# Where weight chunks are staged and when they are requested, added and rooted, in a threshold-attention and feed-forward kernel

## The chip, the cores and the metric

The kernel runs on one core of a Trainium2 chip. The metric is the device time of one execution in microseconds; several executions are taken and their median is given. A profile of one execution stands beside them. Engines are called as the profile calls them: PE (TensorE), DVE (VectorE), ACT (ScalarE), POOL (GpSimd), SP (the engine that issues most transfers). "PEld" is the loading of weights into PE.

## The reference, cut to what matters

```python
# attention: q, k, v are (8, 8, 576, 64) float32, tau a scalar
scores = 1.0 / sqrt(64) * q @ k.transpose(0, 1, 3, 2)
thresh = max(scores, axis=-1) - tau
scores = where(scores >= thresh, scores, -1e9) - max
attn = exp(scores) / (sum(exp(scores)) + 1e-9)
x = (attn @ v), heads joined to (8, 576, 512)
# feed-forward: w_ch1 is (512, 2048), w_ch2 (2048, 512)
mu, var = mean(x), mean((x - mu) ** 2)
xn = (x - mu) / sqrt(var + 1e-6) * g_ln
out = x + maximum(xn @ w_ch1, 0) @ w_ch2
```

The two weight matrices arrive as float64. [...] the kernel takes each value's two 32-bit words apart and makes a float32 of them.

## The kernel before

**Slots.** Attention is done in slots. A batch has 8 heads, two to a partition set, and 9 slots: four for the first 256 rows of each pair of heads, one for the last 64 rows of all, four for the second 256 rows. The loop at L1078 passes 72 slots, numbered n; batch 0 is slots 0 to 8. In a slot PE makes the scores (L402), DVE takes the row maxima (`neg`, L416), POOL the thresholds (`thr`, L420), ACT the exponentials (L429), DVE compares with the threshold, multiplies and sums (L436), and POOL divides by the sum (L452). From slot 6 on (`FIRST`), DVE turns the weights in blocks (L526 for most slots) and SP stores them to DRAM (`scr<-et`, L533 in batch 0, L537 later) and reads them back turned (`em<-scr`, L547, later L551) at the start of the next slot. PE multiplies them with v in part 3 of that next slot (L595, L605). ACT copies these products to `x` (L618) and POOL adds the features up (`sum`, L647) one slot later.

**Feed-forward.** Tokens go in 16 groups of 288. A group's first part makes 16 tiles of `hidden` (`p`, L788, by the helper at L101), each with a relu on ACT (L793). The second part is plain for group 0 (L824, 64 products in four outputs m) and done in seven half-size segments for the others. Two PSUM tiles tagged "ff" take turns for these products, so a product waits for the relu or copy of the last but one. The norm's factor comes from a variance (`var`, L807), Ln and Exp on ACT (L809 to L811), and a correction step on DVE, `root` (L731), which is put on a list `aside` and issued when the list is emptied. Its two scratch tiles in group 0 are `sq[:, 2]` and `sq[:, 3]`, which are tiles 14 and 15 of `hidden`; at L783 `first_part` empties the list before tile 14 is made.

**Order.** The order of every queue is written out by the program: each engine does its instructions in the order in which this Python code issues them. A slot has four places where `second_part` (L999) issues feed-forward steps. It issues as many as fit a share worked out from what is still to be done, and it stops where a weight chunk has not been "carried" yet (L781, L822). POOL's scaling of q (L335) is issued in `turn` (L340), which DVE's transposes of q and k for the next slot belong to.

**Conversion.** `Weights` (L177) brings in 32 chunks of 128 x 512 values, 512 KB each; 0 to 15 belong to w_ch1, 16 to 31 to w_ch2. A chunk goes through these steps:

- `fetch`: SP requests the raw words (L259) into a free piece of SBUF. Pieces lie in regions that are used otherwise later: the unfilled part of `w2`, `hidden`, `x_room`, `y_room`, `et_room`, `stage`, and `e_room[1]`. A piece carries a limit: it may be taken by chunk i only if its limit is above i. Of those that fit, the one with the lowest limit is taken. `wait` says how many ticks ago the piece must have been given back.
- `prepare_to`: ACT writes Abs of the high words to the chunk's final place (L275), and Copies of the low words (L280).
- `begin`: DVE does three masks (L290, L293, L297).
- `carry`: POOL adds the low part (L305) and, for w_ch1, multiplies by g (L308). `carry_all` does this for all chunks begun, last first.

`BEGUN` (L1054) gives for each slot the counts of chunks to be begun after the maxima, after the weights, and at the slot's end. In slot 8, `conversion.fetch(3, ...)` at L1095 requests chunks 29 to 31 early in the slot, ahead of `load_qk` (L1108) and of the store in `turn_blocks` (L1138). At a slot's end, `begin_to(end_at)` and `carry_all()` stand together (L1175, L1176), ahead of the next slot's maxima and thresholds.

Of the kernel before, what the change touches and what calls it, by code (L numbers as in the profile page):

```python
# [8 lines left out]
F32 = mybir.dt.float32  # L9
# [4 lines left out]
AF = mybir.ActivationFunctionType  # L14
# [4 lines left out]
def kernel(  # L19
# [31 lines left out]
    nc = tc.nc  # L51
# [6 lines left out]
    ND = DF // 128  # L58
# [15 lines left out]
    ffn = ctx.enter_context(tc.tile_pool(name="ffn", bufs=2))  # L74
# [6 lines left out]
    eps_sb = consts.tile([128, 1], F32, name="eps_sb")  # L81
# [4 lines left out]
    w2_sb = consts.tile([128, NK, ND, 128], F32, name="w2")  # L86
# [88 lines left out]
    WC = 512  # L175

    class Weights:  # L177
# [13 lines left out]
        def __init__(self):  # L191
            self.chunks = [
                (w1_sb[i][:, c : c + WC], w_ch1[i * 128 : (i + 1) * 128, c : c + WC], i)
                for c in range(0, DF, WC)
                for i in range(NK)
            ] + [
                (
                    w2_sb[:, m, d : d + 4].rearrange("p d c -> p (d c)"),
                    w_ch2[d * 128 : (d + 4) * 128, m * 128 : (m + 1) * 128].rearrange(
                        "(d p) c -> p d c", p=128  # L200
                    ),
                    None,
                )
                for m in range(NK)
                for d in range(0, ND, 4)
            ]
            self.n1 = NK * (DF // WC)
            self.fetched = self.prepared = self.converted = self.begun = self.carried = 0
            self.raw, self.ticks = {}, 2
            flat = lambda t: t.rearrange("p a b -> p (a b)")  # L210

            x_room = ffn.tile([128, NK, TOK], F32, tag="x", bufs=3, name="x_room")
            y_room = ffn.tile([128, NK, TOK], F32, tag="sq", bufs=1, name="y_room")
            et_room = att.tile([128, NB, 128], F32, tag="et", bufs=1, name="et_room")
            stage = self.stage = consts.tile([128, 8, WC], F32, name="stage")

            n1 = self.n1  # L220
            self.free = []
            for t, n, before in (
                (w2_sb.rearrange("p m d c -> p (m d) c"), ND // 2, lambda p: n1 + 2 * p - 6),
                (hidden, 4, lambda p: 10),
                (x_room, 1, lambda p: 2 * n1),
                (y_room, 1, lambda p: 2 * n1),
                (et_room, 2, lambda p: n1 - 3),
                (stage, 4, lambda p: 2 * n1),
            ):
                for p in range(n):  # L230
                    self.free.append((before(p), -1, flat(t)[:, p * 2 * WC : (p + 1) * 2 * WC]))

        def take(self, t):
            t = t.rearrange("p a b -> p (a b)")
            for p in range(2):
                self.free.append((2 * self.n1, -1, t[:, p * 2 * WC : (p + 1) * 2 * WC]))

        def piece(self, i, wait):

# [21 lines left out]
                )  # L261

        def give(self, got):
            self.free.append((got[0], self.ticks, got[2]))

        def words(self, i, t):
            return self.raw[i][2].bitcast(t).rearrange("p (n two) -> p n two", two=2)
# [1 line left out]
        def prepare_to(self, most, lows=True):  # L269

            new = range(self.prepared, max(self.prepared, min(most, self.fetched)))
            for i in new:
                assert all(self.raw[j][0] + 6 > i or self.raw[j][0] == 10 for j in range(self.carried, i))
                dst, top = self.chunks[i][0], self.words(i, F32)[:, :, 1]
                nc.scalar.activation(dst, top, func=AF.Abs)  # L275
            self.prepared = max(self.prepared, min(most, self.fetched))
            while self.converted < (self.prepared if lows else self.begun):
                low, low_in = self.words(self.converted, I32), self.words(self.converted, U32)
                self.converted += 1
                nc.scalar.activation(  # L280
                    low[:, :, 0], low_in[:, :, 0], func=AF.Copy, scale=2.0**-29
                )
# [43 lines left out]
    FIRST = HP + 2  # L326
# [350 lines left out]
    aside, stores, drops = [], [], []  # L677
# [53 lines left out]
    def root(y, x, t):  # L731


        nc.vector.scalar_tensor_tensor(
            out=t, in0=y, scalar=-0.5, in1=y, op0=ALU.mult, op1=ALU.mult
        )
        nc.vector.tensor_mul(t, t, x)
        nc.vector.scalar_tensor_tensor(out=y, in0=t, scalar=1.5, in1=y, op0=ALU.add, op1=ALU.mult)
        rooted.append(y)

    rooted = []
    HT, HD, HM = TOK // 2, ND // 2, NK // 2
# [30 lines left out]
    def first_part(g):  # L773


        xc = centred.pop(g)
        rb = sq = None
        plain = g == 0
        sums_of = differences() if g == 1 else iter(())
        for d in range(ND):  # L780
            while conversion.carried < 4 * (d // 4 + 1):  # L781
                yield 0, 0
            while d == ND - 2 and len(rooted) <= g:  # L783
                run_all(aside)
            p1 = ps_ff.tile([128, TOK], F32, tag="ff", name="p1")
            for c in range(NK):
                product(
                    p1, lhsT=w1_sb[c][:, d * 128 : (d + 1) * 128], rhs=xc[:, c],  # L788
                    start=(c == 0), stop=(c == NK - 1),
                )  # L790
                if c < NK - 1:
                    yield 1, 1
            nc.scalar.activation(hidden[:, d], p1, func=AF.Relu)  # L793
            next(sums_of, None)
            yield 2, 1
            if sq is None and d and (part > 1 or d == ND // 2 - 1):
                squared = d
                sq = hidden[:, ND - NK :]
                nc.scalar.activation(sq, xc, func=AF.Square)
                for c in range(1, NK):  # L800
                    nc.gpsimd.tensor_tensor(out=sq[:, 0], in0=sq[:, 0], in1=sq[:, c], op=ALU.add)
            elif sq is not None and rb is None and (
                d >= squared + (7 if plain else 3) and part > (0 if plain else 1)
                or d == ND - NK - 1
            ):
                var = ps_ff.tile([128, TOK], F32, tag="ff", name="var")
                product(var, lhsT=avg_sb, rhs=sq[:, 0], start=True, stop=True)  # L807
                rb = ffn.tile([128, TOK], F32, tag="rb", bufs=2, name="rb")
                nc.scalar.activation(sq[:, 2], var, func=AF.Identity, bias=eps_sb)  # L809
                nc.scalar.activation(rb, sq[:, 2], func=AF.Ln)  # L810
                nc.scalar.activation(rb, rb, func=AF.Exp, scale=-0.5)  # L811
                aside.append(lambda: root(rb, sq[:, 2], sq[:, 3]))
                yield 1, 1
        for _ in sums_of:
            pass
        return rb
# [171 lines left out]
    def run(n, i):  # L988
        for fn, args in later_calls.pop((n, i), ()):
            fn(*args)  # L990
# [48 lines left out]
    conversion = Weights()  # L1039
    if w_ch1.dtype == I64:  # L1040
        conversion.fetch(2)
    else:
# [10 lines left out]

    BEGUN = [  # L1054
        (0, 0, 1), (2, 2, 3), (4, 4, 5), (6, 6, 7), (8, 8, 9), (10, 10, 11),
        (13, 16, 19), (21, 23, 24), (26, 27, 29), (31, 32, 32), (32, 32, 32),
    ]

    def constants(times):
# [18 lines left out]
    for n in range(NS):  # L1078
# [9 lines left out]
            scale_q(n + 1, loaded[n + 1][0])  # L1088
        rest = exponentials(n)
        es, thr = next(rest)  # L1090
        run(n, 0)
        if n == HP + 2:
            next(rest, None)
        if n >= HP:
            conversion.fetch(3, -1 if n > FIRST else 1)  # L1095
        run_first(stores)
        if n == FIRST:
            convert(masks_at)
# [34 lines left out]
            conversion.carry_all()  # L1133
        box = []
        if blocks_go:
            conversion.fetch(3, wait=0)
            conversion.prepare_to(end_at, False)
            scr = turn_blocks(b, s, es)  # L1138
            if n == FIRST:
                conversion.take(e_room[1])  # L1140
                conversion.fetch(2)
            conversion.carry_all()
            at_quarter(n + 1, 0, lambda b=b, s=s, scr=scr, box=box: box.append(fetch(b, s, scr)))
        else:

            made = turn_weights(s, es, diags)
            for i, at in enumerate(
                (-1, -1, 0, 0)
            ):
                if i == 3 and n + 1 == FIRST:  # L1150
                    at_quarter(n + 1, 0, conversion.prepare_to, BEGUN[n + 1][0], False)
                if i < 3:
                    at_quarter(n + 1, at, next, made)
                else:
                    at_quarter(n + 1, at, lambda made=made, box=box: box.append(next(made)))
# [17 lines left out]
            conversion.prepare_to(BEGUN[n + 1][0] - (n == FIRST - 1))  # L1173
        second_part(n, 3)
        conversion.begin_to(end_at)  # L1175
        conversion.carry_all()  # L1176
        if FIRST <= n < SLOTS:
            conversion.prepare_to(BEGUN[n + 1][0], False)
        if not plain_at(n):
# [42 lines left out]
```

## Time and profile before

| what | value |
|---|---|
| median of 3 runs | 1347.89 us (1347.65 to 1348.77) |
| the profiled execution's own time | 1348.64 us |
| its span in the profile | 1346.9 us |
| mean granted PE clock | 0.995 |
| busy shares of the span | PE 98%, PEld 74%, DVE 65%, ACT 34%, POOL 46% |
| transfers | 213.92 MB, mean 159 GB/s |

The span is the time from the first to the last instruction in the profile, and the execution's own time has 1.7 us around it. A share is an average over the whole span. The conversion of weights lies in the first 160 us of it, where the shares are others; times below count from the span's start. In a row of the timeline the columns are the start in us, the length in us, the engine, the line and operation, output and inputs, and the count of merged instructions; in brackets is the idle time before it and what ended that. In a list of waits they are total us, how often, and the longest. In a table by stretches each engine has its busy us and, in brackets, its instructions.

### The profile page before, as it was taken

To read this page: it belongs to the slowest core of one execution; us is meant where nothing else is said; L and a number is where in the kernel's file an instruction comes from. 1 tells how busy PE (TensorE), PEld (TensorE's weight loads), DVE (VectorE), ACT (ScalarE), POOL (GpSimd) and SP (SyncE) were. 2 spreads that over 40 slices of the span, in tenths; PEclk is the share of its full clock that TensorE was granted. 3 is DMA by queue.
4 is the path that set the end of the run, shared out by engine and by line. 5 is a ranking of instruction groups with operands and counts; after the bars stand their busy time and mean duration, and the time that the engine had idled before them with its cause. 6 is when DMAs were issued, how large, how long until landed. Compare 5 with 4: busy or idle time off the path is not lost.

```text
span 1346.9 us, 40264 instructions
## 1 busy us (share of the span) xinstructions
PE 1315.2 (98%) x17304; PEld 990.6 (74%) x17304; DVE 873.9 (65%) x1544; ACT 458.8 (34%) x995; POOL 624.9 (46%) x836
## 2 busy tenths in 40 slices
PE   8898899999999999999999999999999999999997
PEld 7665557769686786968778696877869677786957
DVE  7899786667666675666756677556756667666112
ACT  5875233232423233232233324233232323323120
POOL 3567456535444444444534454443444445335313
PEclk9999899999999999999999999999999999999999
DMA  8927864557643775447644576447754376443211
GB/s 164 302 75 202 207 176 163 178 150 193 179 150 120 193 200 159 151 156 192 172 149 151 166 179 191 142 143 193 197 171 151 121 199 180 133 156 124 85 19 20
DMA packets 335298, 213.92 MB, mean 159 GB/s; under 512 B 247376, under 2 KB 292688, under 8 KB 327056
## 3 DMA queue, kind: packets, MB, share of 16 engines
q1 hardware_dynamic: 329008, 210.46, 54.5%
q8 instruction: 136, 2.23, 0.7%
q10 hardware_dynamic: 5952, 0.74, 0.4%
q14 instruction: 42, 0.34, 0.1%
q0 software_dynamic: 160, 0.15, 0.1%
HBM read 124.00 MB, written 87.29 MB: 157 GB/s over the span
## 4 chain that ended last, share of the span: by engine, by line
PE 89%; DVE 4%; ACT 2%; DMA 2%; SPq 1%; issue 1%; POOL 1%; ACTq 0%; POOLq 0%; DVEq 0%
PE p L101 36%; PE seg L101 31%; PE sc L402 10%; PE sc L595 8%; PE sc L605 2%; ACT e L429 1%; DVE e L436 1%; PE tp L101 1%; SPq L118 1%; DVE w L297 1%; PE var L101 1%; PE mean L101 1%; DVE neg L416 0%; DMA em<-scr 0%; DVE w L293 0%
## 5 line engine op out<-in xcount | busy, mean ns | idle before, releaser
L101 PE MATMUL p<-xc,w 128*64 128x288 f32 x4096 | 518.9, 409 | 8.4 <-ACT part L880 4.6
L101 PEld LDWEIGHTS p<-xc,w 128*64 128x64 f32 x4096 | 287.4, 137 | 217.8 <-issue 14.9
L416 DVE TENSOR_REDUCE neg<-sc 128x2 f32<-128x1152 f32 x144 | 188.8, 1352 | 286.1 <-PE sc L402 285.6
L452 POOL TENSOR_SCALAR e<-e,den 128x576 f32<-128x576 f32 x264 | 205.8, 792 | 131.3 <-DVE den L441 131.3
L101 PE MATMUL seg<-hidden,w 128*64 128x144 f32 x3840 | 247.9, 287 | 0.0
L101 PEld LDWEIGHTS seg<-hidden,w 128*64 128x64 f32 x3840 | 234.8, 137 | 11.5 <-issue 8.5
L436 DVE SCALAR_TENSOR_TENSOR e<-sc,thr,e 128x576 f32<-128x576 f32 x288 | 222.5, 810 | 19.2 <-POOL thr L420 11.6
L420 POOL TENSOR_SCALAR thr<-neg,low_sb 128x2 f32<-128x2 f32 x144 | 40.3, 280 | 382.6 <-DVE neg L416 381.6
L793 ACT ACTIVATE hidden<-p 128x288 f32<-128x288 f32 x256 | 106.5, 416 | 303.3 <-PE p L101 302.2
L429 ACT ACTIVATE e<-sc,neg 128x576 f32<-128x576 f32 x288 | 197.4, 753 | 2.4 <-DVE neg L416 2.4
L526 DVE STREAM_TRANSPOSE et<-e 128x1152 f32<-128x1152 f32 x118 | 161.0, 1372 | 14.2 <-POOL e L452 13.7
L402 PE MATMUL sc<-kT,qT 64*64 64x384 f32 (+3 forms) x2048 | 140.3, 404 | 2.5 <-DVE e L436 1.6
L595 PE MATMUL sc<-em,v_in 128*64 128x128 f32 (+1 forms) x2368 | 131.5, 265 | 5.9 <-DMA em<-scr 2.8
L595 PEld LDWEIGHTS sc<-em,v_in 128*64 128x64 f32 x2368 | 124.1, 138 | 14.5 <-DVE w L297 3.0
L101 PE MATMUL seg<-hidden,stage 128*64 128x144 f32 x1920 | 123.3, 287 | 0.0
L101 PEld LDWEIGHTS seg<-hidden,stage 128*64 128x64 f32 x1920 | 117.6, 137 | 2.9 <-issue 2.9
L618 ACT COPY x<-sc 128x128 f32<-128x128 f32 x120 | 31.6, 265 | 247.2 <-PE sc L402 175.9
L865 POOL TENSOR_TENSOR hidden<-hidden 128x576 f32<-128x576 f32 x60 | 84.8, 1428 | 52.0 <-ACT hidden L793 42.4
L402 PEld LDWEIGHTS sc<-kT,qT 64*64 64x64 f32 x2048 | 76.3, 133 | 44.1 <-issue 21.3
L880 ACT COPY part<-seg 128x288 f32<-128x288 f32 x74 | 29.8, 403 | 190.6 <-PE seg L101 190.1
L865 DVE TENSOR_TENSOR hidden<-hidden 128x576 f32<-128x576 f32 x60 | 51.2, 887 | 51.5 <-PE seg L101 48.5
L101 PE MATMUL seg<-hidden,e 128*64 128x144 f32 x896 | 61.2, 286 | 0.0
(125 smaller groups left out, 1048.0 us busy)
## 6 DMA issues: line engine op xcount, KB each, us to landing
scr<-et SPq DMA_DIRECT2D x63, 1152.0 KB, 5.0
em<-scr SPq DMA_DIRECT2D x63, 1024.0 KB, 5.8
out_dram<-ot SPq DMA_DIRECT2D x248, 36.0 KB, 3.7
q_in<-in_q_dram SPq DMA_DIRECT2D x120, 72.0 KB, 2.8
er<-scr SPq DMA_DIRECT2D x132, 64.0 KB, 5.1
k_in<-in_k_dram SPq DMA_DIRECT2D x116, 72.0 KB, 3.0
v_in<-in_v_dram SPq DMA_DIRECT2D x28, 256.0 KB, 5.5
w<-in_moe_w_ch_dram SPq DMA_DIRECT2D x10, 512.0 KB, 8.3
```

Of the source, the lines that this page charges most:

```text
L101: nc.tensor.matmul(out[r], lhsT=lhsT[:, r], rhs=rhs, **flags)
L402: nc.tensor.matmul(sc[h][64 * i : 64 * i + 64, at : at + n], lhsT=ql[r] if s == HP else qT[r, half, j * 128 + 64 * i : j * 128 + 64 * i + 64],
L416: nc.vector.tensor_reduce(out=neg[:, i], in_=pairs[h], axis=AXL.X, op=ALU.max, negate=True,)
L420: nc.gpsimd.tensor_scalar(out=thr[:, i], in0=neg[:, i], scalar1=-1.0, scalar2=low_sb, op0=ALU.mult, op1=ALU.add,)
L429: nc.scalar.activation(es[:, i], blocks[i], func=AF.Exp, bias=neg[:, i : i + 1])
L436: nc.vector.scalar_tensor_tensor(out=es[:, i], in0=blocks[i], scalar=thr[:, i : i + 1], in1=es[:, i], op0=ALU.is_ge, op1=ALU.mult, accum_o ...
L452: nc.gpsimd.tensor_scalar(out=es[:, i], in0=es[:, i], scalar1=den[:, i : i + 1], scalar2=1.0, op0=ALU.mult, op1=ALU.mult,)
L526: nc.vector.transpose(et[:, :, 64 * h : 64 * h + 64].rearrange("p n (j c) -> p j n c", j=2), es[:, 2 * h : 2 * h + 2].rearrange("p j (n c) ...
L595: nc.tensor.matmul(dst[64 * h : 64 * h + 64], lhsT=vt[:, h, c, :], rhs=pick(em[:, 2 * j : 2 * j + 2, c], h), start=c == 0 and first, stop= ...
L618: nc.scalar.copy(x_of(2 * b + (s > HP))[:, s % (HP + 1), 128 * j : 128 * j + 128], pv[j])
L793: nc.scalar.activation(hidden[:, d], p1, func=AF.Relu)
L865: eng.tensor_tensor(out=out[at], in0=in0[at], in1=in1[at], op=op)
```

## The change

There are five parts.

1. Pieces have new limits in `w2`: (13, 16, 20, 20, 22, 26, 26, 30) in place of 10, 12, ..., 24. Each piece also gets the number of the first chunk that will be written there (`home`), or 99, and an assertion uses it.
2. `BEGUN` for slots 6, 7 and 9 is changed: chunks 17 and 18 move from the end of slot 6 into slot 7, chunk 20 from after slot 7's maxima to after its weights, chunk 22 to the end of slot 7, chunk 30 of slot 9 to after its weights, chunk 31 to its end.
3. In slot 8 both early requests ask for nothing, and chunks 29 to 31 are requested behind the slot's store. In slot 6 three may be requested behind the store instead of two.
4. From slot 6 on, additions at a slot's end are issued behind the thresholds of the next slot.
5. In group 0 the root has two tiles of its own, of the tag "part", and the list `aside` is no longer emptied ahead of tile 14.

```diff
-                (w2_sb.rearrange("p m d c -> p (m d) c"), ND // 2, lambda p: n1 + 2 * p - 6),
+                (w2_sb.rearrange("p m d c -> p (m d) c"), ND // 2, lambda p: (13, 16, 20, 20, 22, 26, 26, 30)[p]),
...
                 for p in range(n):
-                    self.free.append((before(p), -1, flat(t)[:, p * 2 * WC : (p + 1) * 2 * WC]))
+                    home = 99 if t.shape[-1] != 128 or n != ND // 2 else n1 + 2 * p
+                    self.free.append(
+                        (before(p), -1, flat(t)[:, p * 2 * WC : (p + 1) * 2 * WC], home)
+                    )
...
-                assert all(self.raw[j][0] + 6 > i or self.raw[j][0] == 10 for j in range(self.carried, i))
+                assert all(self.raw[j][3] > i for j in range(self.carried, i))
...
-            while d == ND - 2 and len(rooted) <= g:
+            while d == ND - 2 and len(rooted) <= g and not plain:
                 run_all(aside)
...
-                nc.scalar.activation(sq[:, 2], var, func=AF.Identity, bias=eps_sb)
-                nc.scalar.activation(rb, sq[:, 2], func=AF.Ln)
+                two = [sq[:, c] for c in (2, 3)]
+                if plain:
+                    two = [ffn.tile([128, HM, HT], F32, tag="part", bufs=4, name="two") for _ in two]
+                    two = [t.rearrange("p m t -> p (m t)") for t in two]
+                nc.scalar.activation(two[0], var, func=AF.Identity, bias=eps_sb)
+                nc.scalar.activation(rb, two[0], func=AF.Ln)
                 nc.scalar.activation(rb, rb, func=AF.Exp, scale=-0.5)
-                aside.append(lambda: root(rb, sq[:, 2], sq[:, 3]))
+                aside.append(lambda: root(rb, *two))
...
-        (13, 16, 19), (21, 23, 24), (26, 27, 29), (31, 32, 32), (32, 32, 32),
+        (13, 16, 17), (20, 22, 24), (26, 27, 29), (30, 31, 32), (32, 32, 32),
...
         es, thr = next(rest)
+        conversion.carry_all()
         run(n, 0)
...
-            conversion.fetch(3, -1 if n > FIRST else 1)
+            conversion.fetch(0 if n == FIRST + 2 else 3, -1 if n > FIRST else 1)
...
-            conversion.fetch(3, wait=0)
+            conversion.fetch(0 if n == FIRST + 2 else 3, wait=0)
             conversion.prepare_to(end_at, False)
             scr = turn_blocks(b, s, es)
             if n == FIRST:
                 conversion.take(e_room[1])
-                conversion.fetch(2)
+            if n == FIRST or n == FIRST + 2:
+                conversion.fetch(3)
             conversion.carry_all()
...
         conversion.begin_to(end_at)
-        conversion.carry_all()
+        if n < FIRST:
+            conversion.carry_all()
```

The tuples in `take` and `give` are widened by the same `home` entry.

More of the change, by code (lines that the diff above doesn't have):

```diff
@@ L235, in take @@
             for p in range(2):
-                self.free.append((2 * self.n1, -1, t[:, p * 2 * WC : (p + 1) * 2 * WC]))
+                self.free.append((2 * self.n1, -1, t[:, p * 2 * WC : (p + 1) * 2 * WC], 99))
         def piece(self, i, wait):
@@ L263, in give @@
         def give(self, got):
-            self.free.append((got[0], self.ticks, got[2]))
+            self.free.append((got[0], self.ticks, *got[2:]))
         def words(self, i, t):
```

## The prediction

> **What bounds the kernel now.** I read the page's first part first, then busy time in stretches cut at the row maxima (L416) of each attention slot, then what the TensorE waited for up to 200 us, then the timelines of SP, ACT and POOL around slots 8 and 9. Slot n means one pass of the loop at L1078.
>
> The first part of the page:
> ```profile
> PE 1315.2 (98%) x17304; PEld 990.6 (74%) x17304; DVE 873.9 (65%) x1544; ACT 458.8 (34%) x995; POOL 624.9 (46%) x836
> ```
> TensorE sets the end: 98% busy, and from 175 to 400 us its waits add up to 1.1 us. Only the stage in which weight chunks are converted, slots 0 to 9, has holes. Busy time between the starts of the maxima of slots 7, 8 and 9, the transposes' end in slot 9, and slot 11's scores (start:end length, then busy us and counts for PE, PEld, DVE, ACT, POOL; granted clock, DMA share, GB/s):
> ```profile
> 93.80:102.05 8.25, 8.25 (x90) 4.67 (x88) 8.04 (x11) 4.61 (x10) 7.00 (x6) 1.00 0.70 156
> 102.05:120.84 18.79, 16.16 (x156) 9.36 (x154) 18.38 (x31) 12.51 (x25) 14.97 (x14) 0.91 0.72 205
> 120.84:140.93 20.09, 18.13 (x186) 12.13 (x184) 19.61 (x37) 10.33 (x19) 11.07 (x12) 1.00 0.91 226
> 140.93:159.80 18.87, 13.71 (x118) 8.47 (x116) 17.14 (x31) 5.43 (x10) 13.87 (x15) 0.91 0.80 176
> 159.80:182.60 22.80, 22.26 (x222) 13.94 (x223) 13.28 (x26) 5.91 (x12) 9.89 (x13) 0.93 0.70 185
> ```
> VectorE is busy 98% of slots 7 and 8 and 91% of slot 9: it is the bound there, and TensorE follows. What TensorE waited for:
> ```profile
> PE sc L595 <- DMA em<-scr: 2.8, 1, 2.8
> PE p L101 <- ACT hidden L793: 2.6, 1, 2.6
> PE sc L595 <- DVE o L707: 2.3, 1, 2.3
> PE p L101 <- POOL q_in L335: 1.2, 1, 1.2
> ```
> The 2.6 is slot 7: the relu stands behind exponentials that wait for maxima at 102.05. The 1.2 is slot 8: relus 14 and 15 wait for the root. The 2.3 and 2.8 are slot 8's weights (em) landing; VectorE's o was long done. After these stalls products run slower: 16 (L101) take 3.73 and 3.07 us instead of 2.14, 28 (L595) 3.26 instead of 1.75. All that a faster conversion could give back is some 9 us of waits and 4 of clock.
>
> SP's queue, then ACT and POOL, around slots 8 and 9:
> ```profile
> 131.24 1.67 SPq L259 DMA_DIRECT2D stage<-in_moe_w_ch_dram  x3
> 133.01 5.79 SPq L118 DMA_DIRECT2D q_in<-in_q_dram  x4
> 138.85 3.98 SPq L118 DMA_DIRECT2D k_in<-in_k_dram  x4
> 142.93 4.07 SPq L533 DMA_DIRECT2D scr<-et  x4
> ...
> 150.80 2.18 SPq L547 DMA_DIRECT2D em<-scr  x4
> ```
> ```profile
> 136.52 0.70 ACT L275 ACTIVATE w<-stage 128x512 f32<-128x512 f32 x1 [0.29 <-DMA stage<-in_moe_w_ch_dram]
> ...
> 142.48 2.64 ACT L429 ACTIVATE e<-sc,neg 128x576 f32<-128x576 f32 x4
> ```
> ```profile
> 142.50 1.30 POOL L305 TENSOR_TENSOR w<-w,stage 128x512 int32<-128x512 int32 x1
> 143.79 0.27 POOL L420 TENSOR_SCALAR thr<-neg,low_sb 128x2 f32<-128x2 f32 x1
> 144.02 0.73 POOL L647 TENSOR_TENSOR sum<-sum,x 128x256 f32<-128x256 f32 x1
> 144.74 0.27 POOL L420 TENSOR_SCALAR thr<-neg,low_sb 128x2 f32<-128x2 f32 x1
> 144.99 0.74 POOL L335 TENSOR_SCALAR q_in<-q_in,scl_sb 128x576 f32<-128x576 f32 x1
> ```
> Chunks 29 to 31 are issued at 131.24, ahead of 9.8 us of q and k loads, so slot 8's store goes out at 142.93, 4.9 us after its transposes (137.99). But chunk 29 has landed at 136.5, six us before slot 9's exponentials, which stand behind its Abs in ACT's queue. And POOL's q scale, which VectorE's turn waits for, follows the second threshold at once.
>
> **What the Trainium skill says.** "Perfetto Trace Analysis", section "Tensor Engine Instruction (MATMUL, LD_WEIGHTS)": ACT, DVE and GpSimd are strict FIFOs. The trace agrees: the Abs at 136.52 waited 0.29 for its chunk with nothing passing it. "SBUF — State Buffer", "SBUF: two separate sides": VectorE and GpSimd share a port pair as a lock. The trace agrees in part: a mask op (L290) takes 0.40 us alone, 1.52 beside an addition. "DMA: Bandwidth & Descriptors", "Queues, rings and completion order": each DMA engine takes descriptors in ring order, so a chunk requested behind the store moves behind it. In line with that, q and k issue took 9.8 us behind three chunks and 5.7 us without (154.41 on). "TensorE: Matmul & The Clock Gate", "What's actually happening": idle TensorE drops to half rate. Here it does so after waits of 2.6 and 2.8 us.
>
> **The change, part by part.** I follow VectorE's order; durations are rows of this trace. One conversion is 0.40 + 0.43 + 0.69 = 1.53 us alone, 2.1 beside POOL's scaling (two in 112.41 to 116.66), 3.4 beside additions (two in 95.27 to 102.05). Maxima take 2.6, weights 3.2, transposes 2.6, an addition 1.28, q scale 0.74.
>
> *Pieces.* By the new limits only chunk 24 is fetched earlier, in slot 5 instead of 6; the rest change places. SP has nothing to issue from 65.9 to 93.9 us and covers it: 0. Uncovered, it would be one issue, 0.5 us, up to a landing of 8.3. TensorE's steps per quarter come out the same by the counts (8, 6, 11, 7 in slot 6; 5, 9, 11, 4 in slot 9).
>
> *Slot 7.* Chunks 17 and 18 move behind the maxima, which now start when half the scores are there, 97.9 instead of 102.05. The 2.6 us wait goes. But VectorE owes the same 8 conversions before slot 8's maxima: 100.5 after its own; 17 to 19 with one addition beside them 5.6 (106.1); weights 109.3; 20 and 21 4.6 (113.9); transposes 116.5; 22 and 23 3.5 (120.0). Slot 8 starts 0.8 earlier than 120.84.
>
> *Slot 8.* Maxima until 122.6, second threshold 122.9, then additions 23 and 22 stand ahead of the q scale: 125.5, scale 126.2. VectorE turns k until 123.3 and idles 2.9. Rest of the turn 0.9, root 1.8 (it no longer holds relu 14, which saves TensorE about 1.2, but no longer fills VectorE's wait), 24 and 25 3.1: weights start at 132.0 instead of 129.63. The other 8.4 us of the slot, as before, end the transposes at 140.4 instead of 137.99. The store then goes at once: 2.5 earlier than 142.93, and em lands about 156 to 157 instead of 158.2. That is the gain of the reordering.
>
> *Slot 9.* Chunk 29 is issued after the store's 3.8 us, 144.2. Before, the first of three took 5.3 us to the Abs; behind a store that moves at 170 to 190 GB/s (DMA view of 121 to 124 us, slot 7's) I take 5.8: 150.0. The Abs stands ahead of slot 9's exponentials. Abs 0.6, Copies of 27 and 28 1.2, x copies 0.5: exponentials from 152.3 instead of 142.48. On POOL the sum needs the x copy: 153.0; threshold 153.3; additions 28 and 27 155.9; q scale 156.6. VectorE, with 27 and 28 (143.4), maxima (146.0) and k (146.7) done, idles 9.9. Then turn 0.9, o 0.4, conversion 29 2.2: weights at 160.0 instead of 150.45. Weights 3.2, o's two 0.9, conversion 30 2.8, transposes 2.6: 169.5. Conversion 31, now behind the transposes, 1.5: slot 10's maxima at 171.0 instead of 166.67. VectorE's 6.9 us of idling there before paid for half.
>
> *Slot 10.* Maxima until 173.6; Copy 31 on ACT ends at 174.4, addition 175.7, q scale 176.4, turn 177.3, two o's 178.1, centre 1.5: group 1's first product at 179.6, where the trace has 174.60: +5.0. The same account of the old order gives 175.7, +3.9 between accounts. I take the middle, +4.4. From there TensorE has no hole to lose it in.
>
> The profiled run is 1348.64, its span 1346.9 plus 1.7 around it; the median 1347.89 is 0.75 below that run. Span 1346.9 + 4.4 = 1351.3, run 1353.0, median 1352.3. Bounds: chunk 29 landing at 148 gives +1.8 to +3, at 152 +5.9 to +7; and with every mask op at its time alone, in both orders, the account gives +2.8, with the additions' slowing a third stronger +4.5.
>
> **Rivals.** *Hidden transfer* (18%): chunk 29 lands before 147, so only the q scale and moved conversions remain; the account gives +0.4 to +1.6, 1349. For it: 0.5 MB alone passed at 340 to 370 GB/s, 1.5 us. Against: the store's 1.15 MB at 175 is 6.6 us. *Faster* (8%): em's late landing decides. It costs 2.3 + 2.8 and 2.4 of slow clock; if exponentials of slot 9 are not held, up to 6 come back, 1343. It decides if chunk 29 lands by 144.8, when the first maximum ends, 0.6 after its issue here; against it is every landing in this trace. *Worse* (8%): the late store of slot 9 (169.5) carries its weights' landing into slot 11 and another wait of 3 to 4 us and its slow clock come: 1356 to 1358. Before, landing had 7 us to spare there. *The pieces do nothing* is already in the sum.
>
> **How the numbers follow.** A difference of 0.2%, 2.7 us, is about what a measurement tells from none. Likeliest case, 66%, 1350.6 to 1356; hidden 18%, all within 0.2%; faster 8%; worse 8%. Slower 66 + 8 = 74%. The range drops the faster case and part of the worse: 1347 to 1357.
>
> **What would show it.** Right: a long ACT wait for a stage chunk ahead of slot 9's exponentials, 6 us or so; VectorE's qT (L357) waiting some 3 us in slot 8 and 10 in slot 9; the 2.6 at 105 gone; scr in slot 8 issued near 140; group 1's first product near 179. Wrong: that Abs waiting under 3 us, or slot 9's maxima before 141.

## The result, and the profile after

The changed kernel takes 1355.32 us (median of 5 runs, 1354.74 to 1356.33); the kernel before, run beside it, takes 1348.77. The ratio of the two is 1.0049, 95% interval 1.0034 to 1.0064: slower by about 6.6 us. The forecast was slower by 4.4, with a range that holds the result. The place and the mechanism were right. The size was too small by a third, and the last step of the path was another one than I had named.

Lines of the changed kernel carry higher numbers: L293/L296/L300 are the three masks, L308 the addition, L338 the q scale, L439 the weights, L598 the values, L796 the relu.

The first part of its page, and busy time in the same stretches as before (start:end, length, then PE, PEld, DVE, ACT, POOL, granted clock, DMA share, GB/s):

```profile
PE 1315.0 (97%) x17304; PEld 989.4 (73%) x17304; DVE 873.0 (64%) x1544; ACT 458.9 (34%) x995; POOL 622.8 (46%) x836
```

```profile
120.84:140.93 20.09, 15.48 (x144) 9.70 (x144) 16.80 (x31) 7.21 (x14) 11.93 (x13) 0.92 0.70 150
140.93:159.80 18.87, 14.03 (x124) 7.52 (x113) 7.28 (x14) 7.17 (x14) 4.47 (x6) 0.97 0.88 227
159.80:182.60 22.80, 17.50 (x162) 11.00 (x162) 20.04 (x40) 4.69 (x10) 11.86 (x14) 0.80 0.60 153
```

The work is the same: no engine's busy time moved by more than 2.1 us. In the stretch 140.93 to 159.80, VectorE's busy time fell from 17.14 to 7.28 us, POOL's from 13.87 to 4.47. That was slot 9 in the kernel before (in the changed one slot 9's maxima start at 144.10). VectorE, which bound it, now stands still for more than half of the stretch, and what it has not done there it does from 159.80 on (20.04 instead of 13.28).

What TensorE waited for between 66 and 200 us:

```profile
PE p L101 <- POOL w L308: 4.8, 1, 4.8
PE p L101 <- ACT hidden L796: 4.2, 2, 3.6
PE sc L598 <- issue: 3.8, 1, 3.8
PE sc L598 <- DVE e L439: 1.9, 2, 1.0
```

The 2.6 us of slot 7 is gone, and so are both waits for em. In their place stand a wait of 4.8 for an addition, 3.8 and 0.9 for slot 9's weights, and 3.6 for relu 14 in slot 8. The last of these eats what slot 7 gave: relu 14 no longer waits for the root, but it still stands behind exponentials that wait for slot 8's maxima, and the products behind it start at 124.74, where the kernel before had them at 124.91.

The next rows show where the waits in slot 9 come from: ACT, SP, VectorE, POOL and TensorE of the changed kernel, each in order of time.

```profile
151.99 0.68 ACT L278 ACTIVATE w<-stage 128x512 f32<-128x512 f32 x1 [15.46 <-DMA stage<-in_moe_w_ch_dram]
...
153.99 2.80 ACT L432 ACTIVATE e<-sc,neg 128x576 f32<-128x576 f32 x4
```

```profile
132.84 2.72 SPq L118 DMA_DIRECT2D k_in<-in_k_dram  x4
141.19 3.74 SPq L536 DMA_DIRECT2D scr<-et  x4
145.03 1.53 SPq L262 DMA_DIRECT2D stage<-in_moe_w_ch_dram  x1
...
150.81 4.31 SPq L550 DMA_DIRECT2D em<-scr  x4
```

```profile
153.96 1.36 DVE L419 TENSOR_REDUCE neg<-sc 128x2 f32<-128x1152 f32 x1 [8.51 <-ACT x L621]
155.24 0.77 DVE L356 STREAM_TRANSPOSE kT<-k_in 128x576 f32<-128x576 f32 x1
158.95 0.77 DVE L360 STREAM_TRANSPOSE qT<-q_in 128x256 f32<-128x256 f32 x2 [2.95 <-POOL q_in L338]
...
162.10 0.81 DVE L439 SCALAR_TENSOR_TENSOR e<-sc,thr,e 128x576 f32<-128x576 f32 x1
```

```profile
154.24 0.72 POOL L650 TENSOR_TENSOR sum<-sum,x 128x256 f32<-128x256 f32 x1 [8.41 <-ACT x L621]
155.43 0.27 POOL L423 TENSOR_SCALAR thr<-neg,low_sb 128x2 f32<-128x2 f32 x1 [0.47 <-DMA v_rest<-in_v_dram]
155.66 1.29 POOL L308 TENSOR_TENSOR w<-w,x_room 128x512 int32<-128x512 int32 x1
156.90 1.28 POOL L308 TENSOR_TENSOR w<-w 128x512 int32<-128x512 int32 x1
158.17 0.75 POOL L338 TENSOR_SCALAR q_in<-q_in,scl_sb 128x576 f32<-128x576 f32 x1
```

```profile
158.24 1.68 PE L101 MATMUL p<-hidden,w 128*64 128x288 f32 x8 [4.84 <-POOL w L308]
163.76 0.69 PE L598 MATMUL sc<-em,v_in 128*64 128x128 f32 x4 [3.84 <-issue]
165.37 3.25 PE L598 MATMUL sc<-em,v_in 128*64 128x128 f32 x28 [0.92 <-DVE e L439]
...
181.12 4.59 PE L101 MATMUL p<-xc,w 128*64 128x288 f32 x36 [0.54 <-ACT o L838]
```

Read them in this order. Chunk 29 is requested at 145.03, behind the store, and ACT's Abs of it starts at 151.99 after 15.46 us of idling. Two Copies and the x copies follow, then slot 9's exponentials at 153.99, where the kernel before had them at 142.48. The second maximum stands behind an x copy (8.51 us), the second threshold behind the maximum, additions 28 and 27 behind the threshold, and the q scale behind the additions. Behind the scale come VectorE's turn (2.95), its conversion 29 and slot 9's weights (162.10 instead of 150.45). The profile names v_rest for the second threshold, but the maximum that the threshold reads ends at 155.32, 0.11 before it starts; in experiment 3 the distance is the same, and there the profile names the maximum.

TensorE feels it twice. The product of output m2 with tile 12 of `hidden` waits for the addition of chunk 27. And the values of slot 8 wait for the weights of slot 9: their first four products go when the second weights end (162.83 + 0.81 = 163.64), the other 28 when the fourth do (164.49 + 0.81 = 165.30). The profile calls the first of these waits "issue", but its time is that of the weights, as the second's is, and experiment 3's profile names the weights for both. In the kernel before, TensorE's rows for the same values and for group 1 are these:

```profile
158.23 3.26 PE L595 MATMUL sc<-em,v_in 128*64 128x128 f32 x28 [2.84 <-DMA em<-scr]
...
174.60 4.59 PE L101 MATMUL p<-xc,w 128*64 128x288 f32 x36 [0.54 <-ACT o L831]
```

So 7.1 us are lost at the 28 values. At group 1's first product it is 181.12 against 174.60, 6.5, and that stays to the end: the span is 6.6 longer. Even with the weights on time the values would have been late: the last quarter of em, requested at 153.6 behind the chunks, landed 6.2 later at 159.8, where the kernel before had it at 158.1 (152.5 + 5.6).

### The profile page after: what moved, and what is told of

The parts are those of the page before. It is cut to its first block, busy times and chain, and to the rows that moved or that the text cites. A ratio compares the mean times of both kernels' runs of the same rounds, so it can differ in the third digit from the quotient of the medians.

```text
span 1353.5 us, 40266 instructions
## 1 busy us (share of the span) xinstructions
PE 1315.0 (97%) x17304; PEld 989.4 (73%) x17304; DVE 873.0 (64%) x1544; ACT 458.9 (34%) x995; POOL 622.8 (46%) x836
## 4 chain that ended last, share of the span: by engine, by line
PE 87%; DVE 2%; POOL 1%; SPq 1%; DMA 0%; ACT 0%; issue 0%; POOLq 0%; ACTq 0%; DVEq 0%
PE p L101 36%; PE seg L101 31%; PE sc L405 9%; PE sc L598 8%; PE sc L608 2%; PE mean L101 1%; PE var L101 1%; DMA v_rest<-in_v_dram 0%; DVE e L439 0%; POOL w L308 0%; ACT part L887 0%; SPq L262 0%; SPq L536 0%; DVE w L296 0%; DVE et L529 0%
## 5 line engine op out<-in xcount | busy, mean ns | idle before, releaser
L101 PEld LDWEIGHTS seg<-hidden,w 128*64 128x64 f32 x3840 | 234.9, 137 | 11.5 <-issue 8.5
L439 DVE SCALAR_TENSOR_TENSOR e<-sc,thr,e 128x576 f32<-128x576 f32 x288 | 222.5, 810 | 19.4 <-POOL thr L423 11.6
L796 ACT ACTIVATE hidden<-p 128x288 f32<-128x288 f32 x256 | 106.7, 417 | 302.4 <-PE p L101 302.4
L598 PE MATMUL sc<-em,v_in 128*64 128x128 f32 (+1 forms) x2368 | 131.7, 265 | 5.8 <-issue 3.8
L598 PEld LDWEIGHTS sc<-em,v_in 128*64 128x64 f32 x2368 | 124.2, 138 | 15.0 <-issue 4.7
```

The costliest lines, as they stand in the source:

```text
L101: nc.tensor.matmul(out[r], lhsT=lhsT[:, r], rhs=rhs, **flags)
L439: nc.vector.scalar_tensor_tensor(out=es[:, i], in0=blocks[i], scalar=thr[:, i : i + 1], in1=es[:, i], op0=ALU.is_ge, op1=ALU.mult, accum_o ...
L598: nc.tensor.matmul(dst[64 * h : 64 * h + 64], lhsT=vt[:, h, c, :], rhs=pick(em[:, 2 * j : 2 * j + 2, c], h), start=c == 0 and first, stop= ...
```

## The experiments

Theory A: the late chunk holds ACT, and through ACT slot 9. Theory B: the additions ahead of the q scale are what costs. The text set off under each edit is what I expected before the run. Ratios are to the kernel before, run on the same chip, with 95% intervals; 0.001 is 1.35 us. Times inside a run are those of its one profiled execution.

**1. Chunk 29 early again, 30 and 31 behind the store.** From the changed kernel:

```diff
-            conversion.fetch(0 if n == FIRST + 2 else 3, -1 if n > FIRST else 1)
+            conversion.fetch(1 if n == FIRST + 2 else 3, -1 if n > FIRST else 1)
```

> The changed kernel, with chunk 29 alone requested early in slot 8 again, ahead of the q and k loads; 30 and 31 stay behind the store. Theory A (the Abs of chunk 29, late in landing, holds slot 9's exponentials on ACT): the chunk lands near 136, the wait of 15 us on ACT goes to under 1, slot 9's weights start near 153.5 instead of 162.1, group 1's first product near 174 instead of 181.1, so -7 against the changed kernel: 1346 to 1349, at or just under the kernel before. Theory B (the additions ahead of the q scale are what costs): VectorE's waits of 2.95 us for q in slots 8 and 9 stay and so does the loss: 1353 to 1356.

Measured: 1.0007 (0.9999 to 1.0015). One request of 512 KB, moved, gives back all but 1 us, with the waits of 2.96 us for q still there in slots 8 and 9. B alone falls. But it isn't faster than before either, though the store goes 1.9 us sooner (141.07). The requests of 30 and 31 stand between store and em, em is requested at 150.12 against 150.80, and TensorE waits for em again:

```profile
PE sc L598 <- DMA em<-scr: 4.3, 2, 2.3
```

**2. Abs of chunk 29 behind slot 9's exponentials.**

```diff
-        if FIRST <= n < SLOTS:
+        if FIRST <= n < SLOTS and n != FIRST + 2:
             conversion.prepare_to(BEGUN[n + 1][0], False)
```

> The changed kernel, with the Abs of chunk 29 issued behind slot 9's exponentials instead of ahead of them; the request stays behind the store. Theory A, in the form that it is ACT's order and not the landing itself that costs: chunk 29 still lands near 152, but exponentials start near 145 and VectorE waits for the chunk only at its own conversion; group 1's first product near 175.5 to 176.5, -5 to -6 against the changed kernel, 1348 to 1351. If the landing itself were the bound whatever stands ahead of what: 1353 or more. Theory B: 1353 to 1356.

Measured: 1.0019 (1.0011 to 1.0027). The chunk still lands at 151.8, the exponentials start at 145.27, and 4 us come back, where I had expected 5 to 6. So most of the loss was ACT's order, not the landing itself. What is left seems to be neither A nor B: the 28 values start at 160.52, 2.3 later than before, but slot 9's weights end at 157.89, while em's last quarter, requested at 153.5 behind three chunk requests, lands 6.9 later at 160.4.

**3. Additions ahead of the thresholds again (fourth part undone).**

```diff
         es, thr = next(rest)
-        conversion.carry_all()
...
-        if n < FIRST:
-            conversion.carry_all()
+        conversion.carry_all()
```

> The changed kernel without its fourth part: additions at a slot's end stand ahead of the next slot's thresholds again. Theory A: the chunk still lands late, about 2 us sooner (150) since slot 8's transposes come 2.4 us sooner; VectorE's wait for q in slot 8 goes; in slot 9 additions 27 and 28 no longer follow the held sum, so the loss falls, but some stays: ACT waits 10 us or more for the chunk; between +0 and +4 against the kernel before, 1348 to 1352. Theory B: the whole loss goes, 1348 or less, and the wait on ACT is harmless.

Measured: 1.0005 (0.9997 to 1.0014). ACT is held just as before its Abs (149.37 after 12.46 us), the second maximum still waits 7.25 us for it, and yet nothing is lost. Two rows of TensorE in this kernel say why:

```profile
157.55 0.70 PE L598 MATMUL sc<-em,v_in 128*64 128x128 f32 x4 [5.29 <-DVE e L439]
159.16 3.18 PE L598 MATMUL sc<-em,v_in 128*64 128x128 f32 x28 [0.92 <-DVE e L439]
```

Slot 8's transposes come 2.5 us sooner without the wait for q, so store and chunk do too; in slot 9 no addition follows the held threshold. The weights of slot 9 let the 28 values go at 159.16, within 1 us of where em's landing let them go before (158.23). The late chunk now mostly fills a hole that TensorE had anyway. A and B are both half right: each of the two edits, undone alone, takes the loss away, to within 1 us.

**4. Additions behind the q scale.**

```diff
         es, thr = next(rest)
-        conversion.carry_all()
+        if n < FIRST:
+            conversion.carry_all()
...
                 load_qk(u + 1 if u > 1 else 3)
+        if n >= FIRST:
+            conversion.carry_all()
```

> The changed kernel with the additions moved from behind the thresholds to behind the q scale, so that VectorE's turn does not wait for them. Theory A: VectorE's waits of 2.95 in slots 8 and 9 go, slot 8's store comes 2.5 us sooner and so does the chunk (149.5), but ACT is still held: -2 to -3 against the changed kernel, 1351.5 to 1353.5. Theory B: about the whole loss goes, 1348 to 1349.

Measured: 1.0046 (1.0033 to 1.0058), about 0.4 us better than the change itself, inside the interval. Both expectations missed: A's was 2 to 3 us. The waits for q fall to 0.45 and the 28 values go at 162.52, 2.9 sooner, but TensorE does not keep it. It still waits 4.3 us for addition 27, the 16 products after the values take 3.28 us instead of 2.43, and a second product waits 0.76 for an addition. Of the 2.9 us 1.0 is left at group 1's first product (180.11). So it isn't the q scale alone through which the additions' place costs: behind the held thresholds and the scale they are late for TensorE too.

**5. Only the late request, on the kernel before.**

```diff
-            conversion.fetch(3, -1 if n > FIRST else 1)
+            conversion.fetch(0 if n == FIRST + 2 else 3, -1 if n > FIRST else 1)
...
-            conversion.fetch(3, wait=0)
+            conversion.fetch(0 if n == FIRST + 2 else 3, wait=0)
...
                 conversion.fetch(2)
+            if n == FIRST + 2:
+                conversion.fetch(3)
```

> The kernel before with one part of the change alone: chunks 29 to 31 requested behind slot 8's store. There the Abs of 29 and 30 both stand ahead of slot 9's exponentials, but additions 27 and 28 stand ahead of the thresholds. Theory A with a slack: ACT is held till about 150, slot 9's weights start at 157 to 159, but product m2 d12 does not wait for addition 27; the loss is the weights' end (160 to 162) less em's landing of before (158.2): +2 to +4, 1350.5 to 1352.5. If the late request costs only together with the additions behind thresholds: within 1 us of the kernel before.

Measured: 1.0022 (1.0013 to 1.0030), 3 us. Two Abs (29 and 30) hold ACT there until 151, and the 28 values start at 161.71. Experiment 3 is this edit with parts 1, 2 and 5 of the change, and it costs 0.7 us, 2.3 less; the two intervals barely touch. Part 2 shows in the traces: with chunk 30 begun behind the weights, one Abs and not two stands ahead of the exponentials (150.25 instead of 151.29), and one conversion and not two ahead of the weights (155.89 instead of 158.43).

**6. Only the additions behind thresholds, on the kernel before** (the edit of experiment 3 the other way round):

```diff
         es, thr = next(rest)
+        conversion.carry_all()
...
-        conversion.carry_all()
+        if n < FIRST:
+            conversion.carry_all()
```

> The kernel before with the fourth part of the change alone: from slot 6 on, the additions at a slot's end stand behind the next slot's thresholds, and so ahead of its q scale. Chunks 29 to 31 are requested early as before. Theory A with a slack: VectorE's turn waits 1 to 3 us longer for q in slots 8 and 9, but slot 8's store hangs on SP's queue (142.9) and the values of slot 8 on em, so VectorE's lateness of 3 to 5 us is swallowed by the 6.9 us that it idled ahead of slot 10's maxima: within 1.5 us of the kernel before, ratio 0.9995 to 1.0012. If the additions cost by themselves as much as they cost in the changed kernel (there their place made 6 us): ratio above 1.003.

Measured: 1.0012 (1.0004 to 1.0020), 1.6 us, at the edge of what I had expected. The lateness was not swallowed: the q loads wait for VectorE's turn, and SP's queue passes that on, so the store goes at 145.40 instead of 142.93 and em lands later, as TensorE's timeline of this kernel shows:

```profile
160.56 3.25 PE L595 MATMUL sc<-em,v_in 128*64 128x128 f32 x28 [2.65 <-DMA em<-scr]
```

Late request 3.0, additions 1.6, and the whole change 6.6: the two do more together than apart, by some 2 us. The other parts are in that difference too, and by experiments 3 and 5 they help: on top of the late request and the other parts, the additions' place costs 6.6 - 0.7 = 5.9 us, alone 1.6. The two edits alone together were not run.

**7. Only the root's own scratch, on the kernel before** (fifth part of the change):

```diff
-            while d == ND - 2 and len(rooted) <= g:
+            while d == ND - 2 and len(rooted) <= g and not plain:
...
-                aside.append(lambda: root(rb, sq[:, 2], sq[:, 3]))
+                aside.append(lambda: root(rb, *two))
```

> The kernel before with the fifth part alone, the root on its own scratch. Relus 14 and 15 no longer wait for the root, so the 1.2 us wait of TensorE near 124 falls to 0.3 or less. But TensorE then waits for em of slots 7 and 8, which come when SP's queue lets them: values of slot 8 still near 155 to 158, no difference in time (under 0.5 us). If TensorE's own time bounded these slots: -1.2 us.

Measured: 1.0001 (0.9992 to 1.0009). The wait of 1.2 near 124 falls to 0.57, and TensorE waits as much more for em ahead of slot 7's values (1.40 instead of 0.75). No difference. The two tiles, in the lines left out here, are those of the change.

**8. The request put off further**, behind slot 8's load of v (an amount of lateness against an amount of time):

```diff
-            if n == FIRST or n == FIRST + 2:
+            if n == FIRST:
                 conversion.fetch(3)
...
             load_v((n + 2) // SLOTS * HP + (n + 2) % SLOTS)
+        if n == FIRST + 2:
+            conversion.fetch(3)
```

> The changed kernel with its request for chunks 29 to 31 put off once more, behind slot 8's load of v, which takes SP some 3 us. Theory A: whatever the chunk lands later, slot 9's weights and the values of slot 8 come later, one for one: landing 154.5 to 155.5 instead of 152, +2.5 to +3.5 us against the changed kernel. If the changed kernel is held by the additions alone, or by em: no difference, within 0.7 us.

Measured: 1.0061 (1.0047 to 1.0074), 1357.53, 2.2 above the changed kernel's median, 1.6 by the ratios, and the two intervals overlap. I had expected 2.5 to 3.5. Requested 4.2 us later, the chunk came only 1.0 later, in ACT's timeline of this kernel:

```profile
153.03 0.68 ACT L278 ACTIVATE w<-stage 128x512 f32<-128x512 f32 x1 [14.76 <-DMA stage<-in_moe_w_ch_dram]
```

The weights of slot 9 (163.10) and the 28 values (166.37) followed by 1.0, one for one as expected; about 2 us more are lost between there and group 1's first product (184.05), half of it to a longer time at low clock (16 products in 3.44 us instead of 2.43), the rest to a wait of 1.46 for the centred x:

```profile
184.05 4.59 PE L101 MATMUL p<-xc,w 128*64 128x288 f32 x36 [1.46 <-DVE xc L673]
```

The run also tells what the landing consists of. Requested at 145.03 the chunk needs 7.0 us to the Abs, at 149.22 it needs 3.8. So over 3 us of the 7.0 were not its own transfer but what was still under way ahead of it; that this was the store's data is the likely reading, since the store was the request just before.

**9. The request behind the q and k loads, ahead of the store.** In the changed kernel SP has nothing to issue from 135.56 to 141.19.

```diff
                 load_qk(u + 1 if u > 1 else 3)
+        if n == FIRST + 2:
+            conversion.fetch(3, -1)
```

> The changed kernel, with chunks 29 to 31 requested right behind slot 8's q and k loads, in the 5.6 us in which SP had nothing to issue (135.6 to 141.2), so ahead of the store and behind nothing that delays it. Theory A (late chunk, held ACT, slot 9's weights late, values of slot 8 behind them): the chunk lands at 142 to 143, the exponentials of slot 9 are not held, and em of slot 8 is requested some 3 us sooner than in the kernel with only chunk 29 early, since no chunk stands between store and em: values of slot 8 near 157.5, group 1's first product at 173 to 174, ratio 0.998 to 1.000. Theory C (em's landing no longer matters once slot 9's weights are on time): as with chunk 29 early, ratio 1.0005 or so.

Measured: 0.9982 (0.9975 to 0.9989), 1346.3, as theory A had it. The Abs starts at 139.91 and the exponentials at 145.52; em is requested at 148.70 and the 28 values start at 156.67.

**10. The same, with the additions ahead of the thresholds again** (experiments 9 and 3 together).

> The same, and the additions at a slot's end stand ahead of the thresholds again (fourth part undone), so VectorE's waits of 3 us for q in slots 8 and 9 fall to 1.4 and 0.5. Theory A with both costs real: slot 8's store near 138.7, its em landed by 154 to 155.5, slot 9's weights from about 150, values of slot 8 near 155, group 1's first product at 169.5 to 172: 3 to 5 us faster than the kernel before, ratio 0.996 to 0.998. If the additions' place is worth nothing once the chunk is on time: as the run above.

Measured: 0.9955 (0.9941 to 0.9968), 1342.13. Values and group 1 in TensorE's timeline:

```profile
154.01 1.75 PE L598 MATMUL sc<-em,v_in 128*64 128x128 f32 x28 [1.60 <-DMA em<-scr]
...
167.99 4.59 PE L101 MATMUL p<-xc,w 128*64 128x288 f32 x36 [0.54 <-ACT o L838]
```

Group 1 starts 6.6 us sooner than in the kernel before and 13.1 sooner than in the changed one. The values run at full clock (1.75 instead of 3.25). The place of the additions is worth 0.0027 here, 3.6 us, with the chunk on time.

**11. The request behind the q and k loads, on the kernel before**, and nothing else of the change:

```diff
-            conversion.fetch(3, -1 if n > FIRST else 1)
+            conversion.fetch(0 if n == FIRST + 2 else 3, -1 if n > FIRST else 1)
...
                 load_qk(u + 1 if u > 1 else 3)
+        if n == FIRST + 2:
+            conversion.fetch(3, -1)
```

> The kernel before with its request for chunks 29 to 31 moved behind slot 8's q and k loads, and nothing else of the change. Theory A: q and k loads take 5.5 us instead of 9.8, the store goes right after the transposes (138.2 to 139 instead of 142.9), em of slot 8 lands 3 to 4 us sooner, and as the kernel before waits for just that, 3 to 4 us come back: ratio 0.997 to 0.998. The Abs of 29 and 30 wait for the chunks till 141 to 143, about when slot 9's exponentials are due, so at most 1 us is lost again. If the gain of the last run needed the new counts of begun chunks and the root's own scratch too: ratio above 0.999.

Measured: 0.9954 (0.9942 to 0.9967), 1342.64. SP's queue in this kernel:

```profile
134.00 2.63 SPq L118 DMA_DIRECT2D k_in<-in_k_dram  x4
136.73 1.68 SPq L259 DMA_DIRECT2D stage<-in_moe_w_ch_dram  x3
138.51 5.90 SPq L533 DMA_DIRECT2D scr<-et  x4
```

The q and k loads take 5.0 us instead of 9.8, the store follows the transposes at once, and group 1 starts at 168.21. One request moved beats both kernels, as much as experiment 10 does, and by more than the 3 to 4 us expected: 6.2. So the new counts in `BEGUN`, the new limits and the root's scratch aren't needed for it, and with the chunk on time no gain of theirs shows beside it. What the limits and the counts do alone wasn't tried.

## Why the prediction was right, and where its sizes were off

**What bounds the kernel**: right. TensorE waited 0.6 us from 200 to 420 us of the changed kernel, so a loss in slot 9 reached the end whole.

**Slot 7**: the maxima started at 99.01, not 97.9. They waited for all the scores (96.86 + 2.12 = 98.98), where I had let them start after half. Conversions 20 and 21 took 5.2 us, not 4.6. Slot 8 then started at 121.37 instead of the 120.0 that I gave, so the promised 0.8 us sooner became 0.5 later.

**Slot 8**: right for VectorE. Its wait for q was 2.95 against 2.9, the transposes ended at 141.1 against 140.4. The gain that I put beside it was wrong: em was to land at 156 to 157 and landed at 159.8. It was requested at 150.81, as before (150.80), because the three chunk requests and their 3.6 us took the place that the store had left, and it then took longer to land. The 1.2 us that relu 14 was to save did not come either: the exponentials ahead of it held it nearly as long as the root had (124.18, before 124.40).

**Slot 9**: right in kind. The Abs came at 151.99 instead of 150.0: 0.8 from the later store, 1.2 because behind the store a chunk took 7.0 us where I took 5.8. From there each step kept its distance: weights at 162.10 against 160.0, transposes' end 171.5 against 169.5. I had missed that the second maximum itself stands behind the x copy (8.51 us). It cost only the 0.47 us in which POOL, after the sum, waited for it, since the sum stood behind the same copy.

**Slot 10**: here the step failed. I let the loss reach TensorE through slot 10's maxima and the centred x. It got there sooner, through the addition of chunk 27 and through slot 9's weights ahead of slot 8's values. From the 28 values at 165.37 TensorE then had no hole until its last product of group 0 ended at 180.59 (177.99 + 2.60). In experiment 3 the values and group 1 both come sooner (159.16 and 174.57). The centring of x started at 180.36, and its first quarter was done a moment before the first product at 181.12, so the path that I had named ended within 0.5 us of the one that counted. That the sum did not suffer is luck: nothing in the prediction ties the two. In experiment 8 it is the centred x that comes last.

**The sum**: the terms that were mis-sized are the landing (+2.0) and the correction to the middle between two accounts (-0.6). Without that correction and with the measured landing the account gives 7.0, against 6.5 at that point in the trace. It comes so near by way of the step that did not count.

**The signs**: ACT's wait for the chunk came, but as 15.46 us, not the 6 or so that I wrote (ACT had been idle since 136.5). VectorE waited for q in slot 8 as I said. In slot 9 it idled 11.5 us instead of 10, but 8.5 of them at the second maximum and only 2.95 ahead of qT. The store went at 141.19 and group 1 at 181.12, each later than I wrote by the lateness of the steps above.

**The rivals**: "hidden transfer" fell with the Abs's wait. "Faster" had its mechanism confirmed by experiments 9 to 11: if slot 9's exponentials are not held, em's wait and the slow clock come back, "up to 6". With the additions behind the thresholds 2.4 came (experiment 9), with them ahead 6.1 and 6.2 (10 and 11). But in the changed kernel the chunk didn't land in time for that. "Worse" did not come: slot 9's em was there in time.

## What to carry to other kernels

A request moved out of the way of one transfer lands behind it; look for the instruction that waits for it, and for everything behind that instruction in its engine's queue, which needs nothing of the data. Look for a stretch in which the issuing queue is empty before moving a request past work: here 5.6 us of it lay between the loads and the store. And count slack once: of the two edits that cost 3.0 and 1.6 us alone, either could be undone to take the loss away to within 1 us; together, with the rest of the change, they cost 6.6.

## What the runs showed of the hardware that I had not expected

The same 512 KB took very different times from request to first use, by what was ahead in the queue: 7.0 us to the Abs when requested right behind a 1.15 MB store, 3.8 us when requested 4.2 us later (experiment 8), and 4.1 us ahead of the store, right behind the small q and k loads (experiment 9, 135.79 to 139.91).

How long TensorE's products run slow after a wait does not follow from the wait's length alone. After the same wait of 2.6 us in slot 7 (2.60 to 2.62) the next 16 products took 3.73 us in the kernel before, 3.64 in experiment 6, 2.89 in experiment 5 and 2.16 in experiments 7 and 11. After the values of slot 8 sixteen products took 2.43 us in the changed kernel, whose waits there were 4.8, 3.8 and 0.9, but 3.07 in the kernel before, whose waits were shorter. So the slow products counted at a wait of one profiled execution, here and in the prediction, can differ by 1.5 us in another.
